# Reordering VectorE work, weight loads and the last accumulators at the stage borders of a two-part kernel

## The chip, the cores and the metric

The kernel runs on one core of one Trainium2 chip. The metric is the device time of one execution in microseconds (us). Before the change three runs gave 351.74, 351.79 and 353.08 us, with a median of 351.79 us.

The core has five engines with instruction streams of their own: TensorE (PE, with its weight loads PEld), VectorE (DVE), ScalarE (ACT), GpSimd (POOL), and SyncE, whose queue (SP) issues nearly all DMA transfers. They wait for each other through semaphores. Matmul results go to PSUM, which holds 8 banks; everything else that is computed on lies in SBUF.

## The reference

Two blocks follow each other: a chunked state-space scan, and a feed-forward pair of matmuls with an ELU between them.

```python
# scan: batch 4, heads 8, seq 768, head_dim 32, d_state 16, chunk 32
for c in range(nc):
    cum = np.cumsum(la, axis=-1)
    L = np.exp(cum[:, :, :, None] - cum[:, :, None, :]) * causal
    y[:, :, sl] = einsum('bhij,bhjd->bhid', (C B^T) * L, x) \
                + einsum('bhin,bhnd->bhid', C, state) * np.exp(cum)
    state = decay_full * state + sum(B x decay_from_j)
# bridge: (B,H,S,D) -> (B*S, H*D) = (3072, 256)
h = x @ w_in                      # 256 -> 2048
g = np.where(h > 0, h, np.exp(np.minimum(h, 0)) - 1)
out = g @ w_out                   # 2048 -> 256
```

## The kernel before

**Blocks and stages.** The 3072 tokens are cut into 12 blocks of 256 tokens. Stages handle two blocks at once and are named by their first block: n = 0, 2, 4, 6, 8, 10. A stage has 16 steps (k, or m = 0..15), one for each 128 rows of the 2048 wide hidden layer. Stages 0 and 2 have code of their own (the loop over `j`); stages 4 to 10 are the loop `for n in range(4, NP, 2)`. While stage n does the first feed-forward matmul of its two blocks, it also does the second feed-forward matmul of the stage before it (`second(n - 2)`, advanced by `l2s`), and the scan of the two blocks of the next stage (`stage_scan` and the calls around it). "Border 6" below is the stretch from the last steps of stage 4, where the scan's y for stage 6 is made, to the first steps of stage 6; borders 4, 8 and 10 likewise.

**Words.** From stage 2's second half on, every 32-bit matmul operand is split into a high part, a low part and a sum of scaled parts, called words. `words_of_y` makes those of y: `high_of_y` (L785; y1, on ACT, or ACT and DVE), `low_of_y` (y0, two DVE instructions at L802) and `both_of_y` (y_both, two DVE instructions at L812). `words_of_w`/`low_of_w` make those of a piece of w_in (ACT L767, DVE L768; POOL), `words_of_out`/`low_of_out` those of w_out (ACT L897, DVE L898; POOL). `keep_words` writes a piece's words to DRAM and `load_words` (L757, L758: 512 KB and 256 KB) brings them back in a later stage.

**One step.** `l1_words` runs three passes of two matmuls (L828): into `ps_h` with the high weights and y1, into `ps_h` with the low weights and y0, into `ps_w` with the sums and y_both. Step 0 of a stage begins with `ps_h` and ends with `ps_w`; the other steps begin with `ps_w`. Then ACT reads `ps_w` (L832), DVE adds it into `ps_h` (L840), ACT makes e from that (L849, L850), and DVE makes g one step later (L856, `end_words`).

**Jobs.** The words of g for the second matmul are made in three parts, each in its own step position: `first_of_jobs` (ACT, L911), `second_of_jobs` (DVE, g_low, L912) and `third_of_jobs` (POOL, g_words, L888). Words begun in step k are used by PE (L970) in about step k + 3; those begun in step 13 are the first that the next stage uses. The order of all instructions on an engine is the order of the Python calls, written out by hand (`manual_schedule`).

**Scan ahead.** `decay_mask` (POOL, L544), `turn_part` (part 0 and 1: DVE transposes L468; part 2: `ctm`, POOL L476), `scaled` (POOL, L423), `scores`, `weigh` (DVE), `sums`, `states`, `across`, and in step 13 `inside`, whose small matmuls (L672) make the last of y. Three copies (ACT or DVE, L687/L689) bring each half of it to `yT`.

**The end.** After stage 10, `late_l2` does the second matmul of the last two blocks. Four accumulators (`total`) stand in PSUM, one for each 128 tokens; the two sums of the first three share a bank, and the fourth has a bank of its own for its `ps_high`. PSUM is cut into a pool of 7 rotating banks (`p_a`) and one of a single bank (`p_o`). `put_out` reads both sums (ACT L976, DVE L979) and sends the rows out.

Of the kernel before, what the change touches and what calls it, by code (L numbers as in the profile page):

```python
# [10 lines left out]
F32 = mybir.dt.float32  # L11
# [6 lines left out]
P = 128  # L18
# [15 lines left out]
def kernel(  # L34
# [56 lines left out]
    def psum(shape, name):  # L91
        return p_a.tile(shape, F32, tag="a", name=name)
# [654 lines left out]

    w_kept = tc.dram_tile([DF // CW, P, 3, KC, CW], F32, name="w_kept")

    def keep_words(i):  # L750
        words, low = k_words[i]
        nc.sync.dma_start(out=w_kept[i, :, 0:2], in_=words.bitcast(F32))
        nc.sync.dma_start(out=w_kept[i, :, 2], in_=low.bitcast(F32))
# [63 lines left out]
    def l1_words(n, m, ahead=None):  # L817


        cols = slice(m % 2 * P, (m % 2 + 1) * P)  # L820
        w, w0 = k_words[m // 2]
        w1, both_w, w0 = w[:, 0, :, cols], w[:, 1, :, cols], w0[:, :, cols]
        y1, y0, both_y = y_words[n]
        high, both = psum([P, 2 * BLK], "ps_h"), psum([P, 2 * BLK], "ps_w")
        passes = [(high, w1, y1), (high, w0, y0), (both, both_w, both_y)]
        for ps, lhs, rhs in passes if n > 2 and m == 0 else passes[2:] + passes[:2]:
            for k in range(KC):
                nc.tensor.matmul(  # L828
                    out=ps, lhsT=lhs[:, k], rhs=rhs[:, k], start=k == 0 and lhs is not w0,
                    stop=k == KC - 1 and lhs is not w1)  # L830
        e = ffn.tile([P, 2 * BLK], F32, tag="e", name="e", bufs=2)
        nc.scalar.activation(e, both, ACT.Copy, scale=WORD)  # L832
        first_of_jobs()
        if late:
            end_words()
        if ahead and m == MC - 2:
            high_of_y(ahead)
        if ahead and m == MC - 1:
            both_of_y(ahead)
        nc.vector.scalar_tensor_tensor(  # L840
            out=high, in0=high, scalar=WORD - 1.0, in1=e, op0=ALU.mult, op1=ALU.add)
        if ahead and m == MC - 2:
            low_of_y(ahead)
        second_of_jobs()
        late.append((n, m, high, e))

    def begin_end():
# [104 lines left out]
    def second_of_jobs():  # L952

        if len(begun_jobs) > 1:
            for j in begun_jobs[0]:
                next(j)
        while put_second:
            put_second.pop(0)()
# [4 lines left out]
            for j in begun_jobs.pop(0):  # L963
                next(j)

    def three(both, high, g, w, first, last):

        (g1, g0, both_g), (w0, w1, both_w) = g, w
        for ps, lhs, rhs in ((both, both_g, both_w), (high, g1, w1), (high, g0, w0)):
            nc.tensor.matmul(  # L970
                out=ps, lhsT=lhs, rhs=rhs, start=lhs is both_g and first > 0 or lhs is g1 and first > 1,
                stop=last and lhs is not g1, skip_group_check=True)
# [35 lines left out]

    total = []

    def late_l2(m, t):

        if m == 0:
            both = psum([P, 2, DM], "ps_both")
            total.append((both[:, 0], psum([P, DM], "ps_high") if t == 3 else both[:, 1]))
        three(
            *total[t], [g[:, t * P:(t + 1) * P] for g in g_words[m]],
            [w[:, m % 2] for w in out_words[m // 2]], (m == 0) * (1 + (t == 3)), m == MC - 1)

    def w_take(i, low):  # L1020

# [244 lines left out]

    for j in range(8, 16):
        i = j - 8
        l1_words(2, j)
        if i == 5:  # L1270
            high_of_y(4)
        if i == 6:
            low_of_y(4)
        if i == 7:
            both_of_y(4)
        for p in ((), (6,), (), (7,), (0,), (1,), (2,), ())[i]:
            words_of_w(p)
        if i in (0, 2, 5):
            words_of_out(i // 2)
        for p in ((), (), (6,), (7,), (0,), (), (), ())[i]:  # L1280
            low_of_w(p)
        for p in ((5,), (), (), (6,), (7,), (0,), (), ())[i]:
            keep_words(p)
        if i == 7:
            l2(1, 6)
            l2(1, 7)
        begin_end()
        if i == 0:
            turn_part(5, 2)
            scaled(4, nc.gpsimd)  # L1290
            scaled(5, nc.gpsimd)
        if i < 2:
            load_bc(i + 6)
            l2(1, i)
        if i == 2:
            turn_part(4, 3)
            turn_part(5, 3)
            scores(4, 5)
            sums(4, 5)
            for q in range(4):  # L1300
                weigh_two(4, q)
            l2(1, 2)
            states(4)
            states(5)
            for to in (6, 7):
                load_b(to)
                spread_cum(to)
        if i == 3:
            l2(1, 3)
        if i == 4:  # L1310
            l2(1, 4)
            y = across(4, 5)
            inside(y, 4, 5)
        if i == 5:
            l2(1, 5)
        if i in (4, 6):
            turn_part(6, i // 2 - 2)
        if i in (3, 4, 7):
            low_of_out((3, 4, 7).index(i))
        if i > 4:  # L1320
            begin_decays(6, i + 8)
        third_of_jobs()
    end_words()
    words_of_w(3)
    low_of_w(1)
    low_of_w(2)
    low_of_w(3)
    for i in range(1, 4):
        keep_words(i)

    def stage_scan(n, k):

        m = n + 2
        if k < 2:
            spread_exp(m + k)
        if k == 2:
            load_x(m)
            load_x(m + 1)
        if 0 < k < 5 and (n > 4 or k > 2):
            turn_part(m + (k > 2), (k - 1) % 2)  # L1340
        if k < 3:
            decay_exps(m + (k > 0), (k + 1) % 2)
        if k < 4:
            decay_mask(m + (k > 1), k % 2)
        if k in (4, 5):
            turn_part(m + k - 4, 2)
        if k in (7, 8):
            scaled(m + k - 7, nc.gpsimd)
        if k == 10:
            turn_part(m, 3)  # L1350
            turn_part(m + 1, 3)
        if k in (3, 5) and n > 4:
            load_b(m + (k > 3))
        if k in (6, 7) and m + 2 < NP:
            load_bc(m + k - 4)
        if k > 12 and m + 2 < NP:
            begin_decays(m + 2, k)

    for n in range(4, NP, 2):
# [12 lines left out]
        for k in range(16):  # L1372
            if k < 13 and (n > 4 or k > 4):
                to_begin.append(lambda q=k + 3: job(n - 2, q))
            elif m and k > 12:
                to_begin.append(lambda q=k - 13: job(n, q))
            if not m and k in (4, 6, 8, 10, 12, 14, 15):
                to_begin.append(lambda q=(4, 6, 8, 10, 12, 14, 15).index(k): late_job(q, late_pool))
            l1_words(n, k, m)
            if n == 4 and k in (0, 2, 4, 6, 8):  # L1380
                words_of_out(k // 2 + 3)
            if k in (0, 2, 4, 6, 8, 10) and (k > 2 or n > 4):
                load_words(k // 2 + 2)
            if m and k > 13:
                load_words(k - 14)
            if m:
                stage_scan(n, k)
            begin_end()
            if n == 4 and k in (1, 3, 5, 7, 9):
                low_of_out(k // 2 + 3)  # L1390
            if k not in (11, 12) or not m:
                third_of_jobs()
            if not m:
                l2s(2)
                continue
# [35 lines left out]
        for t in range(4):  # L1431
            late_l2(m, t)
    for t in range(4):
        for m in range(MC - 4, MC):
            late_l2(m, t)
        row, eo = row_of(n + t // 2) + t % 2 * P, small([P, DM], F32, "eo")
        put_out(slice(row, row + P), *total[t], eo)()

# [29 lines left out]
```

## Time and profile before

The profiled execution took 351.47 us, of which the span of the profile is 349.6 us; the other 1.87 us lie around it.

| engine | busy us | share of the span | instructions |
|---|---|---|---|
| PE | 338.1 | 97% | 3742 |
| PEld | 290.0 | 83% | 3742 |
| DVE | 288.5 | 83% | 511 |
| ACT | 258.8 | 74% | 533 |
| POOL | 213.7 | 61% | 242 |

The granted TensorE clock is full in all slices. The share of PE says that at most 11.5 us of the span are without a matmul; a part of that lies in the first 25 us and in the last 3, so only stretches where PE stands idle can give time back, and they have to be looked up one by one. In a timeline line the first number is the start in us from the span's start, the second the time it covers, and the bracket at the end the idle time of that engine just before, with what ended it. "issue" means that the engine waited for nothing that the profile shows.

### The profile page before, as it was taken

What the parts mean: (1) busy time and instruction counts of PE and PEld (TensorE: products, weight loads), DVE (VectorE), ACT (ScalarE), POOL (GpSimd) and SP (SyncE); (2) the same over time, 40 slices, a digit from 0 to 9 for tenths busy, and PEclk for the clock granted to TensorE, in tenths of its full rate; (3) what the DMA queues carried; (4) which work ended last, traced back from release to release, by engine and by line L of the source; (5) the groups of instructions that cost most, each with busy time, mean ns of one, the idle gap of its engine ahead of it and who ended that gap; (6) DMA issues with size and microseconds to landing.
All of it is one profiled execution on the core that took longest, in us unless ns stands there. A gap on an engine that the chain in (4) does not pass through costs nothing.

```text
span 349.6 us, 9629 instructions
## 1 busy us (share of the span) xinstructions
PE 338.1 (97%) x3742; PEld 290.0 (83%) x3742; DVE 288.5 (83%) x511; ACT 258.8 (74%) x533; POOL 213.7 (61%) x242
## 2 busy tenths in 40 slices
PE   8899999999999799998999999999999999999996
PEld 6579888888888588887788888888888889999896
DVE  3898989889988867995999986999986978997951
ACT  4689989598767688765698865698866588897601
POOL 5654554539899495859389658389746255775000
PEclk9999999999999999999999999999999999999999
DMA  8989988474485793655069695169563255060101
GB/s 147 229 223 215 282 190 209 96 126 163 119 204 211 295 243 97 212 122 185 0 189 193 181 302 171 55 182 206 138 198 103 85 186 190 32 197 0 33 0 60
DMA packets 82949, 54.79 MB, mean 157 GB/s; under 512 B 59032, under 2 KB 68568, under 8 KB 82904
## 3 DMA queue, kind: packets, MB, share of 16 engines
q1 hardware_dynamic: 80728, 53.98, 55.8%
q8 instruction: 29, 0.48, 0.5%
q10 hardware_dynamic: 2176, 0.20, 0.5%
q14 instruction: 16, 0.13, 0.1%
HBM read 44.53 MB, written 9.63 MB: 155 GB/s over the span
## 4 chain that ended last, share of the span: by engine, by line
PE 66%; DVE 16%; ACT 6%; issue 4%; POOL 3%; SPq 2%; DMA 2%; DVEq 0%; POOLq 0%; ACTq 0%
PE ps_o L970 13%; PE ps_h L828 11%; PE ps_h L711 11%; PE ps_o L874 10%; PE ps_w L828 6%; PE ps_both L970 5%; DVE g_low L912 4%; DVE ps_h L840 4%; PE ps_y L672 3%; DVE g L856 2%; PE ps_g L577 2%; PE ps_y L654 2%; DMA w<-in_moe_w_in_dram 2%; DVE y_both L812 2%; POOL g_words L888 1%
## 5 line engine op out<-in xcount | busy, mean ns | idle before, releaser
L888 POOL TENSOR_TENSOR g_words<-g_words,g_low 128x512 fp32r<-128x512 f32 x62 | 82.0, 1326 | 54.2 <-ACT e L849 25.2
L970 PE MATMUL ps_o<-o_words,g_words 128*128 128x256 f32 x448 | 84.4, 286 | 0.2
L970 PEld LDWEIGHTS ps_o<-o_words,g_words 128*128 128x128 f32 x448 | 72.4, 190 | 7.4 <-POOL g_words L888 2.6
L849 ACT ACTIVATE e<-ps_h 128x512 f32<-128x512 f32 x72 | 43.1, 599 | 41.0 <-DVE ps_h L840 40.5
L856 DVE SCALAR_TENSOR_TENSOR g<-e,ps_h 128x512 f32<-128x512 f32 x72 | 49.3, 684 | 17.5 <-ACT e L850 15.9
L912 DVE SCALAR_TENSOR_TENSOR g_low<-g_words,g 128x512 fp32r<-128x512 f32 x72 | 63.6, 889 | 0.0
L970 PE MATMUL ps_o<-o_low,g_low 128*128 128x256 f32 x224 | 63.3, 283 | 0.0
L840 DVE SCALAR_TENSOR_TENSOR ps_h<-ps_h,e 128x512 f32<-128x512 f32 x72 | 49.8, 692 | 6.0 <-ACT e L832 4.8
L828 PE MATMUL ps_w<-y_both,w_words 128*128 128x512 f32 x144 | 50.1, 424 | 2.6 <-ACT e L849 2.2
L832 ACT ACTIVATE e<-ps_w 128x512 f32<-128x512 f32 x72 | 42.1, 585 | 12.1 <-PE ps_w L828 11.8
L850 ACT ACTIVATE e<-e 128x512 f32<-128x512 f32 x72 | 45.5, 632 | 2.3
L711 PE MATMUL ps_h<-yT,w_in 128*128 128x256 f32 (+1 forms) x208 | 45.1, 367 | 2.0 <-POOL w_in L254 1.9
L828 PE MATMUL ps_h<-y,w_words 128*128 128x512 f32 x144 | 45.5, 397 | 0.0
L874 PE MATMUL ps_o<-w_out,g 128*128 128x256 f32 x192 | 45.5, 380 | 0.0
L828 PE MATMUL ps_h<-y,w 128*128 128x512 f32 x144 | 44.9, 392 | 0.0
L911 ACT ACTIVATE g_words<-g 128x512 fp32r<-128x512 f32 x72 | 43.6, 623 | 0.0
L711 PEld LDWEIGHTS ps_h<-yT,w_in 128*128 128x128 f32 x208 | 36.3, 190 | 7.6 <-POOL w_in L254 2.7
L970 PEld LDWEIGHTS ps_o<-o_low,g_low 128*128 128x128 f32 x224 | 42.6, 190 | 0.0
L874 PEld LDWEIGHTS ps_o<-w_out,g 128*128 128x128 f32 x192 | 36.1, 190 | 5.4
L828 PEld LDWEIGHTS ps_h<-y,w 128*128 128x128 f32 x144 | 27.0, 188 | 6.7 <-POOL w L888 0.5
L828 PEld LDWEIGHTS ps_h<-y,w_words 128*128 128x128 f32 x144 | 26.6, 188 | 7.1 <-ACT e L832 1.3
L828 PEld LDWEIGHTS ps_w<-y_both,w_words 128*128 128x128 f32 x144 | 23.6, 191 | 6.9 <-DVE y_both L812 2.9
(135 smaller groups left out, 554.9 us busy)
## 6 DMA issues: line engine op xcount, KB each, us to landing
w_words<-w_kept SPq DMA_DIRECT2D x28, 512.0 KB
w<-w_kept SPq DMA_DIRECT2D x28, 256.0 KB
L<-flat SPq DMA_DIRECT2D x20, 256.0 KB
w<-in_moe_w_out_dram SPq DMA_DIRECT2D x8, 512.0 KB
w_kept<-w_words SPq DMA_DIRECT2D x8, 512.0 KB
w<-in_moe_w_in_dram SPq DMA_DIRECT2D x7, 512.0 KB
xr<-in_x_dram SPq DMA_DIRECT2D x24, 128.0 KB
out_dram<-eo SPq DMA_DIRECT2D x18, 128.0 KB
```

The lines of the kernel that those rows point to most:

```text
L711: nc.tensor.matmul(out=ps[:, j, toks], lhsT=w_in[i][:, k, j * P:(j + 1) * P], rhs=yT[n // 2][:, k, n % 2].rearrange("p u i -> p (u i)")[:, ...
L828: nc.tensor.matmul(out=ps, lhsT=lhs[:, k], rhs=rhs[:, k], start=k == 0 and lhs is not w0, stop=k == KC - 1 and lhs is not w1)
L832: nc.scalar.activation(e, both, ACT.Copy, scale=WORD)
L840: nc.vector.scalar_tensor_tensor(out=high, in0=high, scalar=WORD - 1.0, in1=e, op0=ALU.mult, op1=ALU.add)
L849: nc.scalar.activation(e, high, ACT.Relu, scale=-1.0)
L850: nc.scalar.activation(e, e, ACT.Exp, scale=-1.0)
L856: nc.vector.scalar_tensor_tensor(out=g_tile(n, m // 2)[:, m % 2].rearrange("p b i -> p (b i)"), in0=e, scalar=1.0, in1=h, op0=ALU.subtract ...
L874: nc.tensor.matmul(out=o_of[n][:, ts], lhsT=g_of[n // 2, j][:, m % 2, n % 2, ts * P:(ts + 1) * P], rhs=w_out[j][:, m % 2], start=(m == 0 a ...
L888: nc.gpsimd.tensor_tensor(out=out, in0=in0, in1=in1, op=ALU.subtract)
L911: yield nc.scalar.activation(words[:, 0], g, ACT.Copy, scale=NEAR / WORD)
L912: yield nc.vector.scalar_tensor_tensor(out=low, in0=words[:, 0].bitcast(F32), scalar=WORD, in1=g, op0=ALU.mult, op1=ALU.subtract)
L970: nc.tensor.matmul(out=ps, lhsT=lhs, rhs=rhs, start=lhs is both_g and first > 0 or lhs is g1 and first > 1, stop=last and lhs is not g1, s ...
```

## The change

The change has these parts:

1. In `l1_words`, step 15 of a stage that prepares another one: `both_of_y` is called ahead of everything else that DVE does there. The second and third part of the jobs due in step 14 are made in step 15 behind it.
2. Stage 2 now goes through the same path (`l1_words(2, j, 4)`); the words of y for stage 4 are all made in steps 13 to 15, before the words of w pieces 1 and 2. The words of w pieces 2 and 3 move to steps 0 and 1 of stage 4, those of w_out to one step later each, and one transpose of block 6 (`turn_part(6, 1)`) to step 2 of stage 4.
3. A 64-byte DMA, `held`, from `yT` to DRAM is issued by SP in step 14, ahead of the loads of the next stage's first two weight pieces (`load_words(0)` and `load_words(1)`). It reads what the last of the three copies behind `inside` writes.
4. `ctm` moves from steps 4 and 5 to 5 and 7, `scaled` from 7 and 8 to 6 and 8.
5. `late_l2`'s fourth accumulator takes its `ps_high` from `p_o`, and in the last four steps the passes into `both` of all four come before the passes into `high`.

```diff
+    held = tc.dram_tile([1, 16], F32, name="held")
@@ l1_words
+        if ahead and m == MC - 1:
+            both_of_y(ahead)
+            second_of_jobs()
+            third_of_jobs()
         e = ffn.tile([P, 2 * BLK], F32, tag="e", name="e", bufs=2)
         nc.scalar.activation(e, both, ACT.Copy, scale=WORD)
         first_of_jobs()
         if late:
             end_words()
-        if ahead and m == MC - 2:
+        if ahead and m == MC - 2 and n > 2:
             high_of_y(ahead)
-        if ahead and m == MC - 1:
-            both_of_y(ahead)
         nc.vector.scalar_tensor_tensor(
             out=high, in0=high, scalar=WORD - 1.0, in1=e, op0=ALU.mult, op1=ALU.add)
-        if ahead and m == MC - 2:
+        if ahead and m == MC - 2 and n > 2:
             low_of_y(ahead)
-        second_of_jobs()
+        if not ahead or m != MC - 2:
+            second_of_jobs()
@@ three and late_l2 get part=slice(0, 3), the passes to run
-            total.append((both[:, 0], psum([P, DM], "ps_high") if t == 3 else both[:, 1]))
+            total.append((both[:, 0], p_o.tile([P, DM], F32, tag="o", name="ps_high") if t == 3 else both[:, 1]))
@@ stage 2, steps 8 to 15
-        l1_words(2, j)
+        l1_words(2, j, 4)
         if i == 5:
-            high_of_y(4)
-        if i == 6:
-            low_of_y(4)
-        if i == 7:
-            both_of_y(4)
-        for p in ((), (6,), (), (7,), (0,), (1,), (2,), ())[i]:
+            words_of_y(4)
+        for p in ((), (6,), (), (7,), (0,), (), (1,), ())[i]:
             words_of_w(p)
...
-        if i in (4, 6):
-            turn_part(6, i // 2 - 2)
+        if i == 4:
+            turn_part(6, 0)
...
     end_words()
-    words_of_w(3)
     low_of_w(1)
-    low_of_w(2)
-    low_of_w(3)
-    for i in range(1, 4):
-        keep_words(i)
+    keep_words(1)
@@ stage_scan
-        if 0 < k < 5 and (n > 4 or k > 2):
+        if 0 < k < 5 and (n > 4 or k > 1):
             turn_part(m + (k > 2), (k - 1) % 2)
...
-        if k in (4, 5):
-            turn_part(m + k - 4, 2)
-        if k in (7, 8):
-            scaled(m + k - 7, nc.gpsimd)
+        if k in (5, 7):
+            turn_part(m + k // 7, 2)
+        if k in (6, 8):
+            scaled(m + k // 8, nc.gpsimd)
@@ stages 4 to 10
-            if n == 4 and k in (0, 2, 4, 6, 8):
-                words_of_out(k // 2 + 3)
+            if n == 4 and k < 2:
+                words_of_w(k + 2)
+            if n == 4 and k in (2, 4, 6, 8, 10):
+                words_of_out(k // 2 + 2)
             if k in (0, 2, 4, 6, 8, 10) and (k > 2 or n > 4):
                 load_words(k // 2 + 2)
+            if m and k == 14:
+                nc.sync.dma_start(out=held, in_=yT[m // 2][Q:Q + 1, 1, 0, 0, Q:Q + 16])
             if m and k > 13:
                 load_words(k - 14)
...
-            if n == 4 and k in (1, 3, 5, 7, 9):
-                low_of_out(k // 2 + 3)
-            if k not in (11, 12) or not m:
+            if n == 4 and k in (1, 2):
+                low_of_w(k + 1)
+                keep_words(k + 1)
+            if n == 4 and k in (3, 5, 7, 9, 11):
+                low_of_out(k // 2 + 2)
+            if k not in (11, 12, 14) or not m:
                 third_of_jobs()
@@ the end
     for t in range(4):
-        for m in range(MC - 4, MC):
-            late_l2(m, t)
+        for part in (slice(0, 1), slice(1, 3)):
+            for m in range(MC - 4, MC):
+                late_l2(m, t, part)
```

More of the change, by code (lines that the diff above doesn't have):

```diff
@@ L964, in third_of_jobs, with three @@
                 next(j)
-    def three(both, high, g, w, first, last):
+    def three(both, high, g, w, first, last, part=slice(0, 3)):
         (g1, g0, both_g), (w0, w1, both_w) = g, w
-        for ps, lhs, rhs in ((both, both_g, both_w), (high, g1, w1), (high, g0, w0)):
+        for ps, lhs, rhs in ((both, both_g, both_w), (high, g1, w1), (high, g0, w0))[part]:
             nc.tensor.matmul(
@@ L1009, with late_l2 @@
     total = []
-    def late_l2(m, t):
+    def late_l2(m, t, part=slice(0, 3)):
         if m == 0:
             both = psum([P, 2, DM], "ps_both")
-            total.append((both[:, 0], psum([P, DM], "ps_high") if t == 3 else both[:, 1]))
+            total.append((both[:, 0], p_o.tile([P, DM], F32, tag="o", name="ps_high") if t == 3 else both[:, 1]))
         three(
             *total[t], [g[:, t * P:(t + 1) * P] for g in g_words[m]],
-            [w[:, m % 2] for w in out_words[m // 2]], (m == 0) * (1 + (t == 3)), m == MC - 1)
+            [w[:, m % 2] for w in out_words[m // 2]], (m == 0) * (1 + (t == 3)), m == MC - 1,
+            part)
     def w_take(i, low):
```

## The prediction

> **What bounds the kernel now.** The page's first part gives PE 338.1 us of 349.6: PE bounds, and only its idle places can be won. So I read, second, the table by stretches of the time around each border, and third the timeline there.
>
> ```profile
> core 0: us, PE busy (x) PEld busy (x) DVE busy (x) ACT busy (x) POOL busy (x), PEclk, DMA share, GB/s
> 108.00:118.00 10.00, 7.76 (x35) 6.13 (x34) 9.85 (x13) 5.80 (x12) 5.82 (x6) 1.00 0.48 183
> 162.00:170.00 8.00, 6.96 (x102) 6.14 (x96) 6.00 (x11) 4.54 (x9) 4.74 (x4) 1.00 0.30 100
> 215.00:224.00 9.00, 8.50 (x148) 7.43 (x139) 6.03 (x11) 5.98 (x12) 6.07 (x4) 1.00 0.28 97
> 270.00:278.00 8.00, 7.89 (x83) 6.44 (x73) 7.49 (x13) 3.87 (x7) 1.29 (x1) 1.00 0.29 101
> ```
>
> At border 4 PE loses 2.24 us while VectorE is full; at borders 6 and 8 it loses 1.04 and 0.50 us though no engine is full. The timeline of border 4 (PE and DVE rows):
>
> ```profile
> 107.19 1.46 DVE L768 SCALAR_TENSOR_TENSOR w_words<-w_words,w_in 128x512 fp32r<-128x512 f32 x1 [0.85 <-ACT w_words L767]
> 108.57 1.77 DVE L898 SCALAR_TENSOR_TENSOR o_words<-o_words,w_out 128x512 fp32r<-128x512 f32 x1
> ...
> 111.47 1.84 DVE L802 SCALAR_TENSOR_TENSOR y<-y,yT 128x512 fp32r<-128x512 f32 x2
> ...
> 113.23 1.21 DVE L768 SCALAR_TENSOR_TENSOR w_words<-w_words,w_in 128x512 fp32r<-128x512 f32 x1
> ...
> 116.04 1.26 DVE L812 SCALAR_TENSOR_TENSOR y_both<-y,yT 128x512 fp32r<-128x512 f32 x2
> ...
> 116.85 1.00 PE L828 MATMUL ps_w<-y_both,w_words 128*128 128x512 f32 x2 [2.20 <-ACT e L849]
> ```
>
> The bracket names ACT, but PE starts as the first half of y_both ends (116.04 + 1.26/2 = 116.67), and two w pieces, a w_out piece and a transpose stand ahead of it on DVE. Border 6, all engines:
>
> ```profile
> 157.34 0.33 SPq L757 DMA_DIRECT2D w_words<-w_kept  x1
> 163.33 0.67 PE L672 MATMUL ps_y<-M,xr 64*32 64x64 f32 x42 [1.04 <-issue]
> 168.01 0.69 DVE L912 SCALAR_TENSOR_TENSOR g_low<-g_words,g 128x512 fp32r<-128x512 f32 x1
> 168.84 1.29 POOL L888 TENSOR_TENSOR g_words<-g_words,g_low 128x512 fp32r<-128x512 f32 x1 [3.26 <-DVE g_low L912]
> 169.21 2.07 DVE L812 SCALAR_TENSOR_TENSOR y_both<-y,yT 128x512 fp32r<-128x512 f32 x2
> 170.74 0.19 PEld L828 LDWEIGHTS ps_w<-y_both,w_words 128*128 128x128 f32 x1 [0.40 <-DVE y_both L812]
> 171.34 0.19 PEld L828 LDWEIGHTS ps_w<-y_both,w_words 128*128 128x128 f32 x1 [0.41 <-DVE y_both L812]
> 173.73 0.30 PEld L828 LDWEIGHTS ps_h<-y,w_words 128*128 128x128 f32 x2 [0.42 <-ACT e L832]
> ```
>
> Two things are to be seen. y_both takes 2.07 us beside a POOL instruction and PE waits for it; and in the middle of `inside` PE stops for 1.04 us for nothing shown. The end:
>
> ```profile
> 324.33 0.38 PE L970 MATMUL ps_high<-o_words,g_words 128*128 128x256 f32 x1 [0.80 <-DVE g L856]
> 346.23 0.38 ACT L976 ACTIVATE eo<-ps_both 128x256 f32<-128x256 f32 x1 [0.82 <-PE ps_both L970]
> ```
>
> **The change part by part.** Gains are in us.
>
> *Border 4 (parts 1, 2).* To win: the gap 2.20 plus 0.38 that the two matmuls took over their usual 0.62, together 2.58. New DVE order from the end of ACT's y1 at 106.64: y0, o_words, g, ps_h, w_words, y_both. Prices beside a busy POOL, from rows here: y0 twice 1.46 (w_words' row; 1.84 for both is the lowest seen), o_words 1.77; g and ps_h start 0.60 apart. That is 106.7 + 2.92 + 1.77 + 1.20 = 112.6. POOL's next work, two halves of a low w piece of 1.05 each, is over by 111.9, so w_words goes at its short price 0.69 and y_both at 1.26: ready at 114.55. PE comes for it at 114.6 (its `ps_h` passes end then, in the same rows). If both go at contended prices (1.46, 2.07) it is 116.1 and the gain is about 0.7. I take 2.3, bounds 0.7 and 2.58. What was moved away: pieces 2 and 3 are first needed in steps 4 and 6, about 125 and 131 (step 1 at 115.7, 3.1 a step). POOL now makes the low part of piece 2 behind four selects (0.75 each; the first follows ACT's L538, some 0.6 earlier than now, 117.4): 117.4 + 3.0 + 2.1 = 122.5; cover 2.5, and each us beyond would cost one. w_out's words are a step (3.1) later and used from step 8 on. SP passes `keep_words(2)` and `(3)` behind the `ec` and ahead of the `xr` loads; these feed steps 10 and 11.
>
> *`held` (part 3).* In the trace the instruction queue q8 moves 29 packets of 16 KB, about one for each 256 instructions of PE (2 x 3742 / 29 = 258). PE's stop at 162.29 lies on such a boundary. Its packet ran from 160.94 to 161.83, directly as the 768 KB of the load issued at 157.34 ended (transfers busy until 160.95); PE crossed the boundary before, 256 instructions earlier, at about 158.7, and packets that met no load started about 1.05 after theirs. So the load held the packet back by 1.2, which is the stop. At border 8 the load of 211.52 and a packet at 215.15 show the same (stop 0.50). With the load behind the scan both stops go: 1.54; I take 1.4, bounds 0 and 1.54. The price is on SP: `held`, then 512 + 256 KB twice, all wait for the last yT copy, which ends at C = 165.24. With 0.5 for wake-up and one issue, and landings 3.7 and 4.4 after the issue (issue 161.89, landed 165.6 and 166.25), the high and low pieces land at C + 4.2 and C + 4.9. PE starts the pass over the high piece at C + 4.3 and that over the low one at C + 4.7: late by 0.2. It is covered, because the first L970 behind waits for g_words until C + 6.1 anyway (next part). Nothing else stands on SP until the rows go out at 175.47.
>
> [...]
>
> *y_both ahead of g_low and g (part 1), borders 6, 8, 10.* POOL's g_words waits for g_low, so y_both now meets an idle POOL: y0's row without POOL is 1.29 (166.81), against 2.07. All of DVE's work behind is 0.78 earlier, and with it ACT's L849 and L832, whose lateness is the wait of 0.42 at 173.73. But g_low is 1.2 later, its POOL part ends at 171.3, and the first L970 (171.45 now) needs it: the 0.40 and 0.41 are not won on the spot. About 0.5 is won at 173.73. At 180.48, 183.55 and 186.73 PE waits 0.37, 0.41 and 0.53 for g_words, and these hang on the DVE/ACT chain that is 0.78 earlier: so 0.7 each for borders 6 and 8, and 0.45 for border 10, where no such waits follow. Bounds: 0 (POOL keeps its pace) and 0.40 + 0.41 + 0.42 = 1.23 each. If PE waits longer for the first g_words, up to -0.3 each.
>
> *POOL's order (part 4).* At nothing: `ctm` (1.5) only moves behind g_words that PE needs sooner, and the second one still ends at about 196 for scores at 198.3; without that cover it would cost its lateness one for one.
>
> *The end (part 5).* `ps_high` waits for a bank that g (323.59 to 324.28) frees; `p_o`'s bank was last read at 304. Won: 0.80 by PE's row, 1.00 by PEld's; I take 0.85. The last `eo` on ACT can start some 0.7 earlier, and DVE then waits for the last `ps_high` matmul (its end 346.43) instead of for ACT (346.61): 0.15. DVE's words for the tail are done at 337, and the first of the last four steps is needed at 339.7.
>
> *Sum:* 2.3 + 1.4 + 2 x 0.7 + 0.45 + 1.0 = 6.55. The profiled execution took 351.47: 344.9. It lies 0.32 below the median of 351.79, so I predict 345.2. The likeliest case's own range, mostly from border 4 and the chain, is 343.0 to 347.0.
>
> **The rivals.**
> *Chain and POOL keep the pace.* DVE stays contended at border 4 (gain 0.7) and POOL's waits at steps 3 to 5 swallow part 1 elsewhere (0). For it: DVE 9.85 of 10 there, and the POOL waits. Against: POOL idles 4.64 ahead of 118.53. 0.7 + 1.4 + 1.0 = 3.1: 348.7.
> *The stop is not the load's doing.* Then `held` brings nothing and the rest 5.15: 346.6. For it: the trace names no cause. Against: two stops, both right behind such a load, and none at border 10, where the packet came later.
> *The first pieces land too late.* The four transfers, now issued together, share the engines instead of landing in order, and PE waits at the `ps_h` pass of step 0 at three borders. It costs one for one from a landing at C + 5.5 on, and decides from C + 7.7: 3 x 2.2 = 6.6 then outweighs 2.3 + 1.4 + 1.0 = 4.7 by the 1.8 that can be told. With C + 8: 351.8 - 4.7 + 7.5 = 354.6. For it: the loads issued at 176.90 and 180.08 took over 5 beside others. Against: at 161.89 the two landed in order, 0.65 apart.
> *Nothing is won that lasts*, because ACT and DVE lag behind an earlier PE and the banks run out: 351.5. Against it: PE shows no wait between 118 and 162.
>
> **How the numbers follow.** Forecast 0.60; pace 0.18; stop stays 0.10; pieces late 0.06; nothing 0.06. A measurement here tells 0.5%, 1.76 us, from no change: faster means under 350.0, slower over 353.6. Faster: the first three but for 0.03 of the pace case: 0.85; within: 0.09; slower 0.06. With all upper bounds at once the time would be 351.8 - (2.58 + 1.54 + 3 x 1.23 + 1.15) = 342.8; at the other end I take the pace case and 0.5 of the chain's possible loss, 349.2. That leaves out the last two rivals, 0.12.
>
> **What would show it.** Right: at border 4 no gap above 0.5 ahead of `ps_w`; no "issue" stop in L672 at borders 6 and 8; y_both near 1.3; `ps_high` without a wait; the first weight loads issued within 0.6 of the last yT copy. Wrong: a PE wait for a weight load in step 0; y_both at 2 us; POOL waits at steps 3 to 5 longer than now; a "pieces late" case in which PE's new waits exceed 2 us a border.

## The result and the profile after

The changed kernel took 347.91 us (median of four runs, 346.91 to 348.38); the kernel before, run beside it and earlier, 352.44 us (four runs, 351.74 to 354.26). The ratio is 0.986 with a 95% interval of 0.981 to 0.991. The profiled execution took 348.19 us, its span is 346.5 us, so the two profiled executions differ by 351.47 - 348.19 = 3.28 us. The prediction was 345.2 us: the direction was right and the whole range, which took in the rival that VectorE's chain and POOL keep their pace (348.7), held the time. The range of the likeliest case alone, 343.0 to 347.0, did not. Of the forecast gain of 6.6 us only half came by the profiled executions, and two thirds by the medians (4.53). The two profiled executions both ran at the full granted clock (a mean of 1.000 before, 0.999 after); the runs of the kernel before do not all do so (means of 0.990 to 1.000), as the experiment on the tail shows, and its medians are probably higher for it.

The table by stretches, in the four stretches shown of before (PE busy first):

```profile
core 0: us, PE busy (x) PEld busy (x) DVE busy (x) ACT busy (x) POOL busy (x), PEclk, DMA share, GB/s
108.00:118.00 10.00, 10.00 (x46) 8.31 (x45) 8.67 (x11) 5.67 (x11) 4.80 (x4) 1.00 0.35 132
162.00:170.00 8.00, 7.55 (x69) 6.31 (x51) 7.67 (x13) 4.39 (x8) 3.96 (x3) 1.00 0.57 197
215.00:224.00 9.00, 8.52 (x74) 6.97 (x66) 7.91 (x14) 5.24 (x10) 4.28 (x3) 1.00 0.49 176
270.00:278.00 8.00, 6.80 (x44) 5.79 (x43) 7.04 (x12) 5.00 (x10) 2.58 (x2) 1.00 0.65 198
```

At border 4 PE now loses nothing (2.24 before). At border 6 it loses 0.45 in this stretch, with more behind it. At border 8 it loses 0.48, as before (0.50). At border 10, where it had lost 0.11, it loses 1.20. So gains came, and new waits came with them.

Where they lie is told by a ledger: the start of each of the 3742 matmuls in one trace is set against the same matmul in the other (both run them in the same order up to the last four steps), and the places where the lead changes are listed. Lead of the changed kernel over the one before, in us:

| place | change of the lead | lead behind it |
|---|---|---|
| first 25 us and up to border 4 (same instructions) | -0.51 | -0.51 |
| border 4, `ps_w` of step 0 | +2.59 | 2.08 |
| stage 4, `weigh` between steps 9 and 10 | -1.52 | 0.56 |
| border 6, the stop in `inside` | +1.11 | 1.67 |
| border 6, y_both +0.51, then the first g_words -0.92 | -0.41 | 1.26 |
| stage 6, steps 3 to 14 | +0.64 | 1.90 |
| border 8 and the steps behind it | +1.00 | 2.90 |
| border 10, the first two weight pieces | -1.55 | 1.35 |
| border 10, y_both and the steps behind it | +0.83 | 2.18 |
| the tail, `ps_high` | +1.05 | 3.23 |

A ledger rests on one profile of each kernel, and a row of it is good to about 0.1 us.

Border 4 in the timeline (DVE and PE rows):

```profile
107.36 3.72 DVE L804 SCALAR_TENSOR_TENSOR y<-y,yT 128x512 fp32r<-128x512 f32 x2 [0.34 <-ACT y L793]
111.00 1.21 DVE L903 SCALAR_TENSOR_TENSOR o_words<-o_words,w_out 128x512 fp32r<-128x512 f32 x1
...
113.33 0.68 DVE L770 SCALAR_TENSOR_TENSOR w_words<-w_words,w_in 128x512 fp32r<-128x512 f32 x1
113.94 1.28 DVE L814 SCALAR_TENSOR_TENSOR y_both<-y,yT 128x512 fp32r<-128x512 f32 x2
...
115.01 0.76 PE L830 MATMUL ps_w<-y_both,w_words 128*128 128x512 f32 x2
```

y_both is begun at 113.94 instead of 116.04 and PE's `ps_w` has no bracket: the wait of 2.20 is gone. The next loss is 25 us later. First the DVE rows around `weigh` before, then DVE and PE rows of after:

```profile
142.59 1.11 DVE L912 SCALAR_TENSOR_TENSOR g_low<-g_words,g 128x512 fp32r<-128x512 f32 x1
143.63 0.68 DVE L898 SCALAR_TENSOR_TENSOR o_words<-o_words,w_out 128x512 fp32r<-128x512 f32 x1
...
145.43 0.68 DVE L912 SCALAR_TENSOR_TENSOR g_low<-g_words,g 128x512 fp32r<-128x512 f32 x1
146.03 1.41 DVE L586 TENSOR_TENSOR M<-ps_g,L 128x256 f32<-128x256 f32 x4
```

```profile
141.09 1.25 DVE L917 SCALAR_TENSOR_TENSOR g_low<-g_words,g 128x512 fp32r<-128x512 f32 x1
142.26 1.12 DVE L903 SCALAR_TENSOR_TENSOR o_words<-o_words,w_out 128x512 fp32r<-128x512 f32 x1
...
144.51 1.81 DVE L917 SCALAR_TENSOR_TENSOR g_low<-g_words,g 128x512 fp32r<-128x512 f32 x1
146.24 1.41 DVE L586 TENSOR_TENSOR M<-ps_g,L 128x256 f32<-128x256 f32 x4
...
147.13 0.70 PE L830 MATMUL ps_h<-y,w_words 128*128 128x512 f32 x2 [0.69 <-DVE M L586]
```

PE comes 1.5 us earlier than before, but the three instructions shown ahead of M, which make words, now take 1.25 + 1.12 + 1.81 = 4.18 us instead of 1.11 + 0.68 + 0.68 = 2.47, beside a POOL that is busy without a gap (136.24 to 145.77). M starts at nearly the same absolute time (146.24, 146.03 before), and PE's next `ps_h` is released by M: PE waits 0.69 where it had not.

Border 6, DVE, POOL and PE rows of after:

```profile
163.11 1.94 POOL L531 TENSOR_TENSOR L<-L,ncum 128x1024 f32<-128x1024 f32 x1
...
164.21 1.13 DVE L795 TENSOR_SCALAR y<-yT 128x512 fp32r<-128x512 f32 x1
...
168.26 0.68 DVE L917 SCALAR_TENSOR_TENSOR g_low<-g_words,g 128x512 fp32r<-128x512 f32 x1
...
169.09 1.28 POOL L893 TENSOR_TENSOR g_words<-g_words,g_low 128x512 fp32r<-128x512 f32 x1 [4.04 <-DVE g_low L917]
170.42 0.51 PE L975 MATMUL ps_o<-o_words,g_words 128*128 128x256 f32 x2 [0.86 <-POOL g_words L893]
```

There is no "issue" stop in L672 at border 6 any more. PE waits further on, for the first g_words (0.86). At border 8 a stop stays, and in the tail `ps_high` comes without a wait (0.80 before):

```profile
215.47 0.41 PE L672 MATMUL ps_y<-M,xr 64*32 64x64 f32 x18 [0.37 <-issue]
...
321.20 0.28 PE L975 MATMUL ps_high<-o_words,g_words 128*128 128x256 f32 x1
```

Border 10, the SP queue and PE:

```profile
268.85 0.24 SPq L1385 DMA_DIRECT2D held<-yT  x1
269.18 0.34 SPq L759 DMA_DIRECT2D w_words<-w_kept  x1
269.62 1.83 SPq L760 DMA_DIRECT2D w<-w_kept  x1
...
273.87 0.70 PE L830 MATMUL ps_h<-y,w_words 128*128 128x512 f32 x2 [0.52 <-DMA w_words<-w_kept]
275.26 0.71 PE L830 MATMUL ps_h<-y,w 128*128 128x512 f32 x2 [0.68 <-DMA w<-w_kept]
```

The last yT copy ends at C = 268.81 (C is that moment at each border). The high piece, issued at 269.18, is there at C + 4.9 and the low one at C + 6.3 (by the times at which their transfers ended); at borders 6 and 8 they landed at C + 4.0 to 4.1 and C + 4.6 to 4.8. PE waits for both.

### The profile page after: what moved, and what is told of

Read it like the earlier page. It is cut to its first block, busy times and chain, and to the rows that moved or that the text cites. A ratio compares the mean times of both kernels' runs of the same rounds, so it can differ in the third digit from the quotient of the medians.

```text
span 346.5 us, 9640 instructions
## 1 busy us (share of the span) xinstructions
PE 336.4 (97%) x3742; PEld 290.8 (84%) x3742; DVE 288.8 (83%) x511; ACT 258.1 (75%) x533; POOL 214.4 (62%) x242
## 4 chain that ended last, share of the span: by engine, by line
PE 75%; DVE 7%; ACT 5%; SPq 4%; DMA 4%; issue 2%; POOL 1%; DVEq 0%; POOLq 0%; ACTq 0%
PE ps_o L975 18%; PE ps_h L830 14%; PE ps_h L711 11%; PE ps_o L879 11%; PE ps_w L830 8%; PE ps_both L975 6%; DMA w<-w_kept 3%; PE ps_y L672 3%; SPq L184 2%; PE ps_y L654 2%; DVE ps_h L844 2%; PE ps_g L577 2%; DVE g_low L917 1%; ACT e L854 1%; PE ps_st L607 1%
## 5 line engine op out<-in xcount | busy, mean ns | idle before, releaser
L917 DVE SCALAR_TENSOR_TENSOR g_low<-g_words,g 128x512 fp32r<-128x512 f32 x72 | 64.4, 900 | 0.0
L830 PE MATMUL ps_w<-y_both,w_words 128*128 128x512 f32 x144 | 48.7, 419 | 0.0
```

Of the source, the lines that this page charges most:

```text
L830: nc.tensor.matmul(out=ps, lhsT=lhs[:, k], rhs=rhs[:, k], start=k == 0 and lhs is not w0, stop=k == KC - 1 and lhs is not w1)
L917: yield nc.vector.scalar_tensor_tensor(out=low, in0=words[:, 0].bitcast(F32), scalar=WORD, in1=g, op0=ALU.mult, op1=ALU.subtract)
```

## The experiments

Each kernel ran beside the kernel before on the same chip. "Ratio" is to that, with a 95% interval. The profiled times of one kernel differ from its median by up to 1.34 us, and the first 26 us of a run, where all kernels have the same instructions, vary by up to 1.15 us; so effects below 1 us are read from the ledger, place by place, not from the totals.

| kernel | median us | ratio | profiled us |
|---|---|---|---|
| the changed kernel | 347.91 | 0.986 (0.981 to 0.991) | 348.19 |
| no_held | 347.57 | 0.986 (0.981 to 0.991) | 347.66 |
| held_once | 347.22 | 0.985 (0.981 to 0.989) | 346.82 |
| tail_only | 352.18 | 0.999 (0.996 to 1.001) | 352.42 |
| border4_only | 350.31 | 0.993 (0.991 to 0.995) | 350.52 |
| yboth_only | 349.67 | 0.992 (0.990 to 0.995) | 349.55 |
| out_early | 346.47 | 0.984 (0.980 to 0.987) | 345.61 |
| q0_early | 347.13 | 0.985 (0.983 to 0.988) | 348.47 |
| both_early | 346.57 | 0.983 (0.981 to 0.985) | 345.92 |
| y1_act | 344.68 | 0.978 (0.974 to 0.981) | 344.23 |
| y1_act_q0 | 345.71 | 0.980 (0.976 to 0.983) | 345.92 |
| pool_old | 346.77 | 0.983 (0.980 to 0.986) | 346.86 |
| y1_pool_old | 344.78 | 0.978 (0.976 to 0.980) | 345.53 |

### `held` taken away (no_held)

```diff
-            if m and k == 14:
-                nc.sync.dma_start(out=held, in_=yT[m // 2][Q:Q + 1, 1, 0, 0, Q:Q + 16])
```

> The changed kernel without the small copy `held`, so that the first two weight pieces of a stage are loaded as step 14 and 15 are written, as before; all else changed. Theory 1 (the load holds back PE's instruction packet, and the late pieces are what PE waits for at border 10): the stop in the middle of `inside` at border 6 is back, 0.9 to 1.1 us, with a packet that starts over 2 us after its boundary; at border 8 the stop stays near 0.5; at border 10 the two waits for w_words and w (0.5 and 0.7 by PE's rows) are gone. Net against the changed kernel's 348.2 us: between -0.9 and 0, so 347.3 to 348.2. Theory 2 (the stop belongs to where the instructions happen to lie, not to the load): no stop at border 6, border 10 gains as above: 346.7. Theory 3 (the waits of border 10 are not from `held`): they stay, and the stop comes back: 349.2.

The stop is back. SP, PE, POOL and DVE rows of no_held at border 6:

```profile
156.92 0.33 SPq L757 DMA_DIRECT2D w_words<-w_kept  x1
...
162.81 0.67 PE L672 MATMUL ps_y<-M,xr 64*32 64x64 f32 x42 [0.94 <-issue]
163.23 1.93 POOL L531 TENSOR_TENSOR L<-L,ncum 128x1024 f32<-128x1024 f32 x1
...
165.36 0.42 DVE L793 TENSOR_SCALAR y<-yT 128x512 fp32r<-128x512 f32 x1
...
170.88 0.51 PE L973 MATMUL ps_o<-o_words,g_words 128*128 128x256 f32 x2 [0.17 <-POOL g_words L891]
```

The trace also times the packets of the instruction queue q8: 29 of 16 KB in the profiles of before and after, one for 258 of PE's 2 x 3742 instructions. That they are PE's, with 256 instructions each, is the author's estimate from these counts; no row marks where a packet's instructions begin. For the packet at border 6 and the one at border 8, counted from the boundary so estimated (the start of the 128th matmul ahead of the place of the stop, since 128 matmuls and their weight loads are 256 instructions):

| kernel | border 6: packet starts after | PE stops | border 8: packet starts after | PE stops |
|---|---|---|---|---|
| before | 2.25 | 1.04 | 1.69 | 0.50 |
| yboth_only (loads as before) | 2.50 | 1.28 | 1.58 | 0.46 |
| no_held | 2.19 | 0.94 | 1.50 | 0.35 |
| the changed kernel | 0.92 | none | 1.60 | 0.37 |
| held_once (loads as before at border 8) | 0.86 | none | 1.53 | 0.21 |

At border 6 theory 1 is shown: with the weight load ahead of it the packet starts 2.2 to 2.5 late and PE stops, without it 0.9 and PE doesn't; theory 2 falls. At border 8 the packet starts 1.50 to 1.69 late with the load and 1.60 without it, so the load is not its cause; what is stays open. The traces of all fourteen kernels agree that the stop goes with the packet's lateness: 2.2 to 2.5 gives 0.94 to 1.28 (border 6 of the five kernels that load there as before), 1.4 to 1.7 gives 0.18 to 0.50 (border 8 of nine kernels), and what starts earlier, at border 6 (0.8 to 1.4) and at border 8 (0.9 to 1.25), gives 0.07 at most. Among the last is border 8 of border4_only, with the loads as before. At border 10 the waits for the weights are gone.

What the missing stop is worth is another matter. In the ledger of the changed kernel against no_held, `held` wins 1.02 at the stop, then loses 0.69 at the first g_words, and 0.66 and 0.92 at border 10's weights, of which 0.39 comes back behind them; with 0.07 won in between it comes out 0.8 behind. Where the 0.69 goes can be read in the rows: without the stop yT is ready earlier, and y1 on DVE now meets POOL's long L instruction, whose time had hardly moved: 1.13 us instead of 0.42, 0.71 more. The totals (347.57 against 347.91) can't tell the two kernels apart.

### `held` at border 6 alone (held_once)

```diff
-            if m and k == 14:
+            if n == 4 and k == 14:
```

> The changed kernel with `held` in stage 4 alone (border 6), not in stages 6 and 8. Theory 1 (`held` pays at border 6 alone): border 6 as in the changed kernel, without a stop; border 8 keeps about its 0.5; the weight waits of border 10 are gone, which gives 1.2 to 1.8: 346.4 to 347.0. Theory 2 (the waits of border 10 follow from DVE's order, y_both ahead of g_low and g): another wait stands in their place and less than 0.5 is won: 347.7 to 348.2.

Border 6 as in the changed kernel, and at border 10 the ledger gains 0.66 + 0.91 and gives back 0.38 to the wait for g_words that follows: 1.19 us, theory 1. The profiled 346.82 us lies in the forecast 346.4 to 347.0; the median of 347.22 is not told apart from the changed kernel's. Every kernel below has `held` at border 6 alone, if nothing else is said.

### The tail alone (tail_only)

The kernel before with part 5 of the change alone.

> The kernel before with the change's fifth part alone: the fifth last accumulator in the free bank, and the last four steps split in two passes. Theory: the wait of 0.80 ahead of ps_high is gone and the last eo no longer ends the kernel: -0.85 to -1.15, so 350.3 to 350.6 against the profiled 351.5. Rival (the wait moves to the next bank or to the weights of the tail): less than 0.3 won, 351.2 or more.

The ledger moves by +1.06 at `ps_high`, as expected. The total missed the forecast, for a reason elsewhere: the profiled run lost 1.66 us in the first step of stage 4 by the ledger, behind border 4's gap, where the table by stretches shows a granted clock of 0.66 (0.5 for 3.41 us, from 119.06 on):

```profile
118.00:123.00 5.00, 5.00 (x16) 4.06 (x17) 3.82 (x6) 4.70 (x10) 3.77 (x5) 0.66 0.79 311
```

The mean granted clock of each run bears this out. All ten runs of tail_only have 0.993 to 0.995; the profiled one, with this one drop, has 0.995. Of the eighteen runs of the kernel before beside them nine have that too, with a median of 353.18 us, and nine have 0.998 to 1.000, with 352.05. Like against like the tail is worth 353.18 - 352.18 = 1.00 us, as forecast.

Over all experiments the mean is at or below 0.995 in 27 of 46 runs of the kernel before, in ten of ten of tail_only and in two of six of yboth_only, which all keep the gap at border 4. In the kernels without that gap it is 0.998 or more in all 56 runs. So border 4's moves very likely take this drop away as well, a gain that the forecast did not count. That the gap is its cause is not shown beyond this, and its place was seen in one trace alone.

### Border 4 alone (border4_only)

The kernel before with part 2 of the change, and y_both ahead of DVE's other work for stage 4's y alone.

> The kernel before with the moves around border 4 alone: y_both(4) ahead of the other VectorE work, w pieces 2 and 3 and w_out's words later, one transpose later; no `held`, the old order at borders 6, 8 and 10, the old order of POOL's scaled products, the old tail. Theory 1 (a gift of the moves themselves: VectorE keeps its absolute pace at steps 8 to 10 of stage 4, now with w_out's words in them, so PE catches up with it): +2.4 to +2.7 at border 4 and -1.2 to -1.6 lost at steps 8 to 10, so net -0.9 to -1.5: 350.0 to 350.6 against 351.5. Theory 2 (the loss at steps 8 to 10 belongs to the new order of POOL's scaled products): nothing is lost there, 348.8 to 349.1.

Theory 1: +2.58 at border 4, then -0.61 and -0.51 at `weigh`, so -1.13 in all, a little less than the 1.2 to 1.6 forecast. M and PE around `weigh`:

```profile
144.18 1.81 DVE L914 SCALAR_TENSOR_TENSOR g_low<-g_words,g 128x512 fp32r<-128x512 f32 x1
145.91 1.41 DVE L586 TENSOR_TENSOR M<-ps_g,L 128x256 f32<-128x256 f32 x4
...
146.80 0.70 PE L828 MATMUL ps_h<-y,w_words 128*128 128x512 f32 x2 [0.28 <-DVE M L586]
```

M starts at 145.91 here, at 146.03 before and at 146.24 after: the absolute time of DVE hardly moves, whatever PE has won. (This run and the one of after are 0.5 to 0.6 us late from their first 25 us on; counted without that, M moved by 0.3 to 0.7 while PE had won 2.6.)

### y_both first at borders 6, 8 and 10 alone (yboth_only)

The kernel before with part 1 of the change for n > 2 and the jobs of step 14 moved to step 15.

> The kernel before with the new order of VectorE at borders 6, 8 and 10 alone: y_both ahead of g_low and g; the loads, border 4, POOL's order and the tail as before. Theory 1 (the chain is won, but the first g_words is then what PE waits for): y_both takes 1.3 instead of 2.07 us, the waits of 0.40, 0.41 and 0.42 at the borders become one wait for POOL's g_words of 0.5 to 0.8, and the waits of 0.37, 0.41 and 0.53 at steps 3 to 5 of stage 6 shrink: between -0.5 and -1.5 over the kernel, 350.0 to 351.0 against 351.5. Theory 2 (POOL keeps its pace): y_both is shorter but PE's time is the same within 0.3: 351.2 to 351.8.

Theory 1, with more than was forecast. DVE and PE rows at border 6:

```profile
168.80 1.29 DVE L812 SCALAR_TENSOR_TENSOR y_both<-y,yT 128x512 fp32r<-128x512 f32 x2
170.00 0.69 DVE L915 SCALAR_TENSOR_TENSOR g_low<-g_words,g 128x512 fp32r<-128x512 f32 x1
...
172.18 0.50 PE L973 MATMUL ps_o<-o_words,g_words 128*128 128x256 f32 x2 [0.18 <-POOL g_words L891]
```

y_both takes 1.29 instead of 2.07, and the ledger wins 0.97, 0.91 and 0.52 from the three borders to the steps behind them: 2.40 us (the stop at border 6, 0.24 longer in this profile, is not counted). A further 0.56 comes at the tail, where the wait ahead of `ps_high` shrank from 0.80 to 0.24; the change wins that by part 5 too, so the two don't add. The profiled 349.55 us lies below the range of 350.0 to 351.0 forecast.

### One piece of w_out's words earlier (out_early)

```diff
+OUT_AT = (2, 4, 5, 6, 10)
...
-            if n == 4 and k in (2, 4, 6, 8, 10):
-                words_of_out(k // 2 + 2)
+            if n == 4 and k in OUT_AT:
+                words_of_out(OUT_AT.index(k) + 3)
...
-            if n == 4 and k in (3, 5, 7, 9, 11):
-                low_of_out(k // 2 + 2)
+            if n == 4 and k - 1 in OUT_AT:
+                low_of_out(OUT_AT.index(k - 1) + 3)
```

> The changed kernel with `held` in stage 4 alone (profiled at 346.8 us on its own), and one piece of w_out's words made in step 5 of stage 4 instead of step 8, where the changed order had put it; its low part on POOL moves from step 9 to 6. Theory 1 (VectorE, filled by that piece and slowed beside POOL's o_low, holds PE at `weigh` in steps 8 to 10): the waits of 0.36, 0.45 and 1.09 us ahead of ps_g and ps_h near 142 to 147 shrink by 0.8 to 1.4 together: 345.4 to 346.0. Theory 2 (`weigh` itself and the banks of ps_g set the pace there, whatever stands on VectorE): less than 0.3 is won, 346.5 or more.

DVE's rows ahead of `weigh` in out_early:

```profile
140.62 1.20 DVE L918 SCALAR_TENSOR_TENSOR g_low<-g_words,g 128x512 fp32r<-128x512 f32 x1
...
143.30 0.79 DVE L918 SCALAR_TENSOR_TENSOR g_low<-g_words,g 128x512 fp32r<-128x512 f32 x1
144.01 1.41 DVE L587 TENSOR_TENSOR M<-ps_g,L 128x256 f32<-128x256 f32 x4
```

No o_words stands there, g_low takes 0.79 instead of 1.81, M starts at 144.01, and PE's wait ahead of `ps_h` is gone. Against held_once the ledger wins 0.21 + 0.85 = 1.06 at this place and nothing is lost behind it: theory 1. What border 4 had lost in stage 4 was DVE's and POOL's work in the way, not `weigh` itself.

### The first g_words of a stage earlier (q0_early, both_early)

```diff
-            elif m and k > 12:
-                to_begin.append(lambda q=k - 13: job(n, q))
+            if m and k in (12, 14, 15):
+                to_begin.append(lambda q=(12, 14, 15).index(k): job(n, q))
```

> The changed kernel with `held` in stage 4 alone, and the first g_words of each following stage begun in step 12 instead of 13, so that its VectorE and POOL parts are done before the last part of the scan; the second and third begin in steps 14 and 15 as before. Theory 1 (after the change the first second-layer matmul of a stage waits for POOL's g_words, which now starts behind y_both): the waits of 1.45, 0.82 and 0.64 us by PE's weight loads at the three borders go, worth 1.2 to 2.0 together: 344.8 to 345.6 against 346.8. Theory 2 (the second g_words or VectorE's chain is then as late, or the extra g_low in step 13 holds up the scan): less than 0.5 is won.

> The last two edits together on the changed kernel with `held` in stage 4 alone. If the two waits are independent the gains add: 343.4 to 344.8 us. If VectorE's pace through stage 4 takes one of them back, no better than the better of the two.

Theory 2, both times: the wait for the first g_words goes (+1.08 in the ledger at border 6), and a wait for ACT's e of 0.58 one step later and the waits for g_words at steps 3 to 5 are there in its place. Behind the first 26 us q0_early's ledger ends 1.3 behind held_once's; the medians (347.13 and 347.22) can't tell the two apart. In both_early against out_early it is +0.99 and then -0.65, -0.30 and -0.24; it ends 0.18 behind. The rows of q0_early say why:

```profile
159.44 3.39 DVE L917 SCALAR_TENSOR_TENSOR g_low<-g_words,g 128x512 fp32r<-128x512 f32 x2
...
165.20 2.12 POOL L531 TENSOR_TENSOR L<-L,ncum 128x1024 f32<-128x1024 f32 x1
166.04 2.43 DVE L804 SCALAR_TENSOR_TENSOR y<-y,yT 128x512 fp32r<-128x512 f32 x2
...
172.72 0.73 PE L830 MATMUL ps_h<-y,w_words 128*128 128x512 f32 x2 [0.58 <-ACT e L838]
```

The two g_low take 3.39 us beside POOL, and POOL's L instruction, which comes 2 us later behind the second g_words, now runs beside y0, which takes 2.43 instead of 1.28: DVE's chain at the border is longer, not shorter.

### y1 on ScalarE (y1_act, y1_act_q0)

On out_early; y1_act_q0 has the edit of q0_early as well.

```diff
-        if n == 4:
+        if n > 2:
             nc.scalar.activation(y1[:, 0], y[:, 0], ACT.Copy, scale=NEAR / WORD)
```

> The kernel with `held` in stage 4 alone and w_out's fifth piece early (profiled at 345.6 us), and the first half of y1 at borders 6, 8 and 10 made on ScalarE, as border 4 has it, instead of on VectorE, where it took 1.21 us beside POOL. Theory 1 (VectorE's chain y1, y0, y_both, g_low sets when POOL's first g_words comes): g_low ends 0.7 to 1.1 earlier, and the waits of 1.37, 0.84 and 0.65 us for g_words shrink by 1.2 to 2.2 together: 343.4 to 344.4. Theory 2 (ScalarE's e and the banks of the next step are then as late, as they were when the first g_words was begun a step earlier): less than 0.5 is won.

> The same with the first g_words of each following stage begun in step 12. Alone that edit won nothing, since the wait for ScalarE's e one step later took the place of the wait for g_words. Theory 1 (e was late through VectorE's chain, which is now shorter): better than the kernel with y1 on ScalarE alone by 0.3 to 1.0 us. Theory 2 (e is late through VectorE's extra g_low in step 13, or through POOL): no better, or worse by up to 0.5.

ACT, DVE and PE rows of y1_act at border 6:

```profile
162.55 0.62 ACT L794 ACTIVATE y<-yT 128x512 fp32r<-128x512 f32 x1
...
163.21 1.29 DVE L805 SCALAR_TENSOR_TENSOR y<-y,yT 128x512 fp32r<-128x512 f32 x2 [0.28 <-ACT y L794]
...
165.62 0.69 DVE L918 SCALAR_TENSOR_TENSOR g_low<-g_words,g 128x512 fp32r<-128x512 f32 x1
...
167.80 0.50 PE L976 MATMUL ps_o<-o_words,g_words 128*128 128x256 f32 x2 [0.26 <-POOL g_words L894]
```

The wait for g_words at border 6 falls from 0.94 by PE's row in out_early to 0.26, +0.67 in the ledger, and nothing behind it takes that back. By the weight load's rows the wait at border 8 falls from 0.84 to 0.65 and the one at border 10 stays (0.65 and 0.69): y1 had taken only 0.64 and 0.42 there in out_early, so there was little to win. The profiled 344.23 us lies in theory 1's range, but its mechanism shows at one border of three, and 0.3 of the gain stands in the first 26 us. Beginning the first g_words earlier loses again (345.71 against 344.68), more than the 0.5 that theory 2 allowed.

y1_act has the lowest median of the study, with y1_pool_old (344.78) not told apart from it: 344.68 us, ratio 0.978 (0.974 to 0.981), against the changed kernel's 0.986 (0.981 to 0.991).

### POOL's order put back (pool_old, y1_pool_old)

On the changed kernel with `held` at all borders, and on y1_act:

```diff
-        if k in (5, 7):
-            turn_part(m + k // 7, 2)
-        if k in (6, 8):
-            scaled(m + k // 8, nc.gpsimd)
+        if k in (4, 5):
+            turn_part(m + k - 4, 2)
+        if k in (7, 8):
+            scaled(m + k - 7, nc.gpsimd)
```

> The changed kernel with POOL's scaled products and their transposes in their old steps (4, 5 and 7, 8). Theory 1 (that part is worth nothing: M at steps 8 to 10 comes at the same time either way): 348.2 within 0.4, the wait ahead of ps_h near 147 stays within 0.2 of 1.09 us. Theory 2 (the two products one behind the other hold back the g_words that PE needs): a wait for POOL of 0.5 or more at steps 8 to 10 of the stages, 349 or more.

> The fastest kernel so far (`held` in stage 4 alone, w_out's fifth piece early, y1 on ScalarE; profiled at 344.2 us) with POOL's scaled products back in their old steps. Theory 1 (what the old order won on the changed kernel, 0.4 ahead of ps_h near 147, came from VectorE being full there; with w_out's piece gone it is no longer): within 0.4 of 344.2. Theory 2 (the old order frees POOL for PE's g_words in every stage): 0.5 to 1.0 less, 343.2 to 343.7, with the wait of 0.48 for g_words near 182 gone.

On the changed kernel the old order is 0.42 ahead at `weigh` (the wait ahead of `ps_h` by the weight load's row is 0.69, not 1.09); theory 1 had the wait unchanged, so both theories missed. The rest of what pool_old's profile is ahead comes from the first 25 us, and from border 10's weights, which came less late (at C + 4.9 and C + 5.6); no run ties the latter to POOL's order. Border 8's stop is gone in pool_old too, but the 0.63 won there is lost again to the first g_words. On y1_act the old order does nothing at any place: a difference of 1.15 stands in the first 26 us and 0.13 at border 8's stop.

## Why the prediction was right in direction and too large

*Border 4, 2.3 forecast.* Right at the place: 2.59 in the changed kernel, 2.58 alone. The sum had y0 at 2.92 and o_words at 1.77; they took 3.72 and 1.21, together 0.24 more, and w_words and y_both went at their short prices, as it had them. (Its lower bound of 0.7 set the end of y_both, 116.1, against PE's start behind the first half; end against end, 117.30, it is 1.2.) What failed is the step that counted the moved work as covered and set against the rival "nothing is won that lasts" that PE shows no wait between 118 and 162. It showed none because PE was late. Once PE came 2 us earlier, DVE and POOL at `weigh`, which kept their absolute time, set its pace, and 1.52 of 2.59 went back. border4_only shows that border 4's moves alone cause 1.13 of that; out_early, that taking one piece of w_out's words out of the way wins 1.06 back.

*`held`, 1.4 forecast.* This step failed, though its mechanism was half right. The load does hold back the packet at border 6 (it starts 2.2 to 2.5 late behind the load, 0.8 to 1.4 late without it), and 1.04 was the size of the stop. It is not the cause at border 8 (0.50 forecast, none won). And the price, "late by 0.2, covered by the first L970 waiting for g_words", was wrong in two ways (its 0.5 for wake-up and one issue was an estimate; at border 10 it was 0.37, 269.18 - 268.81): at border 10 the pieces landed at C + 4.9 and C + 6.3 instead of C + 4.2 and C + 4.9, which cost 1.19 with what came back behind it; and "g_words until C + 6.1" became C + 6.85 (170.42 - 163.57), since y1 slipped under POOL's L instruction. By the ledger `held` costs 0.8 instead of winning 1.4, and this is the largest error of the sum. The rival "the first pieces land too late" came true at one border of three, well short of its 2.2 at each. It was also the one of the prediction's signs of being wrong that showed: a wait of PE for a weight load in step 0.

*y_both ahead of g_low and g, 1.85 forecast.* Right mechanism, size too small: 2.40 alone, of which border 6 has 0.97 and border 8 0.91 where 0.7 each was put. In the changed kernel border 6 lost it again at once to g_words, as the forecast said it would on the spot.

*POOL's order, nothing forecast.* -0.42 at `weigh` in the changed kernel, nothing once DVE has room there.

*The end, 1.0 forecast.* 1.06 alone, 1.05 in the changed kernel.

*The sum.* The single parts, read from the ledgers, give 2.58 - 1.13 + 2.40 - 0.80 - 0.42 + 1.06 = 3.69. The ledger of the changed kernel gives 3.23, and 0.51 more without the slower first part, which no edit touched: 3.74. That the two agree this well is partly chance, since each term is good to 0.1. What is missing of the forecast 6.55 is `held` (2.20) and the loss at `weigh` (1.55, with POOL's share), less what border 4 and y_both brought above their forecasts (0.28 and 0.55). That the whole range held the time is owed to the low rivals in it, not to the sum.

## What to carry to other kernels

An engine that shows no wait may only be late enough to have none (at `weigh` 1.52 of border 4's 2.59 us went back): before counting a gain as lasting, look in the next 30 us for the engines whose work is not tied to it, and ask when their last result would be needed if the bound engine came earlier. When a transfer is put behind a wait to keep it out of another one's way, every place that runs this code pays the price (1.19 us at border 10), so put it only where the stop was seen. And where removing one wait exposes another of nearly the same size, shorten the chain both hang on (here y1 on DVE), not the order of their last links.

## What the runs showed of the hardware

- A DVE instruction that takes 0.42 us alone (y1) took 1.13 to 1.26 at border 6 beside POOL's 1.94 us L instruction, and two that take 1.28 together (y0) took 2.43 beside an L instruction of 2.12 and 3.72 at border 4 beside a POOL busy from 103.77 to 112.81; the same y1 on ACT took 0.62 beside an L of 1.93 (y1_act). No run here shows by what DVE is held up.
- In one profiled run (tail_only) the granted clock fell to 0.5 for 3.41 us (a mean of 0.66 between 118 and 123 us), behind a PE gap of 2.44 us, and the ledger shows 1.66 us lost there, while the mean clock of that run is 0.995; nearly the same gap (2.28) in the profiled run of yboth_only had no such drop. By the mean clocks of the timed runs the drop comes and goes from run to run of the same kernel (0.995 or less in 27 of 46 runs of the kernel before), and only in kernels with that gap (none of 56 runs of those without it).
- One issue on SP took 1.83 us where the other loads at the changed kernel's borders took 0.34 to 0.42 (border 10, the second of four loads), and the load ahead of it landed 0.8 to 0.9 later than at the other borders (C + 4.9 against C + 4.0 to 4.1). Why isn't settled; in pool_old the second piece's issue took 0.37, the third's 1.02, and the high piece still landed at C + 4.9.
